# Two neighbouring rows of w_out to a partition, and every second column of w_in as the stationary operand

## The chip, the cores and the metric

The kernel runs on one core of one Trainium2 chip. The metric is the device time of one execution in microseconds (us). The time before is the median of five runs.

## What is computed

The first half is a gated linear attention over a sequence of 768, for 4 × 8 batches and heads of width 48; its output, as 3072 tokens of 384 numbers, goes through a two-layer perceptron with a squareplus in the middle. The change touches the perceptron only:

```python
# q, k, v, f_logit: (4, 8, 768, 48) float32; w_in: (384, 2048); w_out: (2048, 384)
f = 1.0 / (1.0 + np.exp(-f_logit))
for t in range(S):
    state = f[:, :, t, :, None] * state + np.einsum('bhd,bhe->bhde', k[:, :, t], v[:, :, t])
    y[:, :, t] = np.einsum('bhd,bhde->bhe', q[:, :, t], state)
x = y.transpose(0, 2, 1, 3).reshape(B * S, H * D)      # (3072, 384)
h = x @ w_in                                           # (3072, 2048)
g = 0.5 * (h + np.sqrt(h * h + 4.0))
out = g @ w_out                                        # (3072, 384)
```

## The kernel before

**Tiles of work.** The 3072 tokens are cut into 12 tiles, p = 0 to 11, of 256 tokens, three tiles to a batch. A tile has two halves, cc = 0 and 1, of 128 tokens. For each tile the kernel loads f, q, k and v (line 175), builds decay factors from f (exponentials, logarithms and cumulative sums with line 284's and 290's matmuls), scales q and k into a tile `qk` of fp16 (the products of line 142), transposes it into `qkT` (TensorE's line 391 for the first tiles, a transposing transfer at line 374 for tiles 4 to 11), computes scores (line 415), masks them into `pm` (line 430), updates the state (lines 443, 453, 469) and adds up the attention's output `y` in PSUM (lines 493, 502). `y` is copied to fp16 and transposed into `xT` (lines 517 or 526).

**First layer of the perceptron.** `xT` has for each half three blocks of 128 features by 128 tokens. The piece `m1.p.m` (line 542), for m = 0 to 7, computes 256 of the 2048 hidden columns: two groups, a = 0 and 1, of 128 columns each. A group is three matmuls that add up in PSUM; each has a 128x128 block of w_in as its stationary operand and 256 tokens as its moving operand. So a tile has 48 of these matmuls, all tiles 576, and each has a weight load of its own. The weights stand in four SBUF tiles `win`, of shape 128 x 3 x 512 in fp16, and group a takes the 128 contiguous columns from m % 2 * 256 + a * 128 on.

**Squareplus.** ScalarE squares h (line 551) and takes the root (line 557); VectorE adds half of h to it and writes the tile `g` (line 567), 128 hidden units to the partitions, 16 groups jn = 2m + a, 256 tokens.

**Second layer.** The piece `m2.p.cc n4` (line 579) runs four of the 16 groups jn; the 16 add up in one PSUM bank to 128 tokens by 384. The stationary operand is a 128x128 block of `g`, the moving operand the 384 columns of the 128 rows of w_out that belong to jn: `wout[jn // 2][:, jn % 2, :]`. There are 384 such matmuls. The result is copied to SBUF (`os`, line 139 on VectorE or line 137 on ScalarE) and stored (line 599).

**Weights.** w_in comes in four transfers of 384 KB of fp16 (line 148) and w_out in eight of 192 KB (line 153, pieces wo0 to wo7). Both are issued by GpSimd and turn float32 of memory into fp16 on the way. Transfer i of w_out brings rows 256 i to 256 i + 255: partition p gets row 256 i + p as j = 0 and row 256 i + 128 + p as j = 1. So a partition reads two runs of 384 numbers, 1536 bytes each, that lie 128 rows apart.

**What sets the order.** The order of all pieces is one list written out in the program, with the engine (and the PSUM banks) of each; on each engine the pieces run in that order. The loads of inputs, the transposing transfers and all stores but two of the last tile are issued from SP's queue in the list's order, so a store that waits for its data holds back the loads behind it. The w_out pieces stand in GpSimd's order between products and casts for tiles 2 to 5, and the first use of w_out is m2.0.00. Waits between pieces follow from the tiles that they read and write; buffers are reused in a ring of fixed depth for each name.

Of the kernel before, what the change touches and what calls it, by code (L numbers as in the profile page):

```python
# [126 lines left out]
def describe(nc, W, ctx_tiles, aps):  # L127
    q, k, v, f_logit, moe_w_in, moe_w_out, out = aps
    T, sb, ps, K = ctx_tiles
# [20 lines left out]

    for i in range(8):
        def wout(e, b, i=i):
            nc.gpsimd.dma_start(out=K["wout"][i], in_=moe_w_out[i * 256:(i + 1) * 256, :].rearrange("(j p) n -> p j n", p=128))

        W.add(f"wo{i}", "P", wout, makes=[f"wout{i}"], dma=("w", 1.26), cost={"P": 0.74})

    for p in range(NP):
        parts = [(0, 4), (4, 8)] if p in FINE else [(0, 8)]
        xs = range(len(parts))
        n = 384 // len(parts)  # L160
# [217 lines left out]
        if p not in XBAR:  # L378
            for x, (h0, h1) in enumerate(parts):
# [15 lines left out]
                for cc in range(2):  # L395
# [5 lines left out]
                    m = (j1 - j0) * 256  # L401
# [135 lines left out]
        for m in range(8):  # L537
            def m1(e, bk, m=m, p=p):
                T["h", p, m] = ps(bk[0], [128, 2, 2, 128], FP32)
                for a in range(2):  # L540
                    for j in range(NJ):
                        nc.tensor.matmul(out=T["h", p, m][:, a], lhsT=K["win"][m // 2][:, j, m % 2 * 256 + a * 128:m % 2 * 256 + a * 128 + 128],  # L542
                                         rhs=T["xT", p][:, :, j, :], start=(j == 0), stop=(j == NJ - 1))
            W.add(f"m1.{p}.{m}", "T", m1, reads=[f"xT{p}", f"win{m // 2}"], makes=[f"h{p}.{m}"], uses=[("xT", p)],
                  banks=[f"h{m}.{p}"], mode="F", cost={"T": 0.665})
            r, a = divmod(m, 2)

            def sq(e, bk, m=m, r=r, a=a, p=p):
                if ("hsq", p, r) not in T:
                    T["hsq", p, r] = sb("hsq", 4 * p + r, [128, 2, 512], FP16)  # L550
                nc.scalar.activation(out=T["hsq", p, r][:, a], in_=T["h", p, m].rearrange("p a c t -> p (a c t)"), func=AF.Square, scale=1.0)  # L551
            W.add(f"sq{p}.{m}", "A", sq, reads=[f"h{p}.{m}"], makes=[f"hsq{p}.{r}"], uses=[("bank", f"h{m}.{p}"), ("hsq", 4 * p + r)],
                  cost={"A": 0.585})
            if a == 1:
                def rt(e, bk, r=r, p=p):
                    T["r16", p, r] = sb("r16", 4 * p + r, [128, 2, 512], FP16)
                    nc.scalar.activation(out=T["r16", p, r], in_=T["hsq", p, r], func=AF.Sqrt, scale=0.25, bias=1.0)  # L557
                W.add(f"rt{p}.{r}", "A", rt, reads=[f"hsq{p}.{r}"], makes=[f"r16{p}.{r}"], uses=[("hsq", 4 * p + r), ("r16", 4 * p + r)],
                      table="s", cost={"A": 1.065})

        for m in range(8):
            r, a = divmod(m, 2)
# [167 lines left out]
```

## Time and profile before

| | |
|---|---|
| median of 5 runs | 196.72 us (196.11 to 200.51) |
| the profiled execution's own time | 197.05 us |
| its span, from the first to the last instruction | 194.8 us |
| granted TensorE clock, mean of the span | 0.987 |
| TensorE matmuls busy, of the span | 174.2 us |
| VectorE, ScalarE, GpSimd busy | 152.2, 156.0, 117.7 us |
| packets of transfers, bytes | 80505, 32.87 MB |
| of these from GpSimd's queue | 3872, 3.34 MB |
| w_out, from issue to landing | 7.1 us (median of 8) |

PE is TensorE's matmuls and PEld its weight loads, DVE is VectorE, ACT ScalarE, POOL GpSimd and SP SyncE, which only issues transfers; a q behind an engine's name is its instruction queue. A matmul's recorded duration runs from its start to the end of the pipeline, so durations of neighbouring matmuls overlap: the pace of a stream is the difference of the starts. The same holds for weight loads. A wait for several things is put down to the one that came last.

### The profile page before, as it was taken

The numbers are of one execution on the slowest core, as the hardware profiler recorded it, in microseconds if no ns is written. First come the engines' busy times: TensorE is split into PE (matmuls) and PEld (weight loads), VectorE is DVE, ScalarE is ACT, GpSimd is POOL, SyncE is SP. The second block draws the span as 40 slices with busy tenths as digits, with TensorE's granted clock in tenths as the row PEclk, the third lists the DMA queues.
The fourth block names the chain that finished last, engine by engine and source line by source line (L and its number), as shares of the span: only waits on it lengthen the run. The fifth ranks groups of instructions, "written<-read, shape, count | busy, mean of one in ns | idle before, by whom it ended". The sixth has DMA issues, their size and how long they took to land.

```text
span 194.8 us, 5593 instructions
## 1 busy us (share of the span) xinstructions
PE 174.2 (89%) x2287; PEld 125.7 (65%) x2287; DVE 152.2 (78%) x278; ACT 156.0 (80%) x250; POOL 117.7 (60%) x150
## 2 busy tenths in 40 slices
PE   0359997989999999899999899999987999999990
PEld 0236764767667766787677667777755777777660
DVE  5699869999989998779988978789755885664540
ACT  4568689899999979979999888997757779779800
POOL 5329889899999867787987999399700100000020
PEclk9999998799999999999999999999999999999998
DMA  5999999999968999999999979991989083000605
GB/s 141 276 260 249 234 242 247 215 254 246 201 151 196 211 201 242 197 261 225 230 190 227 129 142 227 200 205 28 96 141 184 3 69 89 13 0 0 162 13 152
DMA packets 80505, 32.87 MB, mean 169 GB/s; under 512 B 73888, under 2 KB 80448, under 8 KB 80480
## 3 DMA queue, kind: packets, MB, share of 16 engines
q1 hardware_dynamic: 76608, 29.17, 76.3%
q0 software_dynamic: 3872, 3.34, 10.6%
q8 instruction: 18, 0.29, 0.7%
q14 instruction: 7, 0.06, 0.1%
HBM read 25.17 MB, written 4.72 MB: 153 GB/s over the span
## 4 chain that ended last, share of the span: by engine, by line
PE 55%; DMA 12%; DVE 11%; POOL 8%; issue 4%; ACT 4%; SPq 3%; DVEq 0%; POOLq 0%
PE ps L579 22%; PE ps L542 20%; DVE pm L430 4%; DMA q<-in_q_dram 3%; DMA k<-in_k_dram 3%; POOL qk L142 3%; DMA v<-in_v_dram 2%; DMA xT<-y 2%; PE ps L493 2%; DVE g L567 2%; PE ps L391 2%; DMA out_dram<-os 2%; PE ps L415 2%; PE ps L284 2%; PE ps L502 2%
## 5 line engine op out<-in xcount | busy, mean ns | idle before, releaser
L542 PE MATMUL ps<-xT,win 128*128 128x256 f16 x576 | 75.6, 278 | 2.3 <-DVE os L139 0.9
L567 DVE SCALAR_TENSOR_TENSOR g<-ps,r 128x512 f16<-128x512 f32 x96 | 62.2, 682 | 15.1 <-ACT r L557 15.0
L579 PE MATMUL ps<-wout,g 128*128 128x384 f16 x384 | 71.4, 326 | 0.1
L551 ACT ACTIVATE hsq<-ps 128x512 f16<-128x512 f32 x96 | 54.1, 592 | 16.7 <-PE ps L542 16.3
L542 PEld LDWEIGHTS <-win 128*128 128x128 f16 x576 | 55.5, 99 | 15.1 <-issue 1.7
L557 ACT ACTIVATE r<-hsq 128x1024 f16<-128x1024 f16 x48 | 50.7, 1057 | 2.3 <-DVE g L567 1.0
L579 PEld LDWEIGHTS <-g 128*128 128x128 f16 x384 | 36.3, 98 | 19.8 <-issue 0.4
L430 DVE TENSOR_TENSOR pm<-ps,mask 128x512 f16<-128x512 f32 x48 | 31.1, 682 | 6.3 <-PE ps L415 6.2
L142 POOL TENSOR_TENSOR qk<-q,ea 128x384 f16<-128x384 f32 x22 | 22.6, 1049 | 0.2
L599 POOL DMA_DIRECT2D out_dram<-os x2 | 1.1, 576 | 35.2 <-DVE os L139 35.2
L142 POOL TENSOR_TENSOR qk<-k,ep 128x384 f16<-128x384 f32 x18 | 17.6, 997 | 0.2
L142 POOL TENSOR_TENSOR UT<-UT 128x384 f32<-128x384 f32 (+1 forms) x11 | 11.4, 1041 | 8.3 <-DVE UT L232 8.2
L284 PE MATMUL ps<-hl,tri 128*128 128x384 f16 (+1 forms) x34 | 9.1, 377 | 6.6 <-ACT hl L259 5.5
L142 POOL TENSOR_TENSOR sn<-st,gs 128x384 f16<-128x384 f32 x6 | 5.0, 829 | 14.0 <-DVE st L469 11.8
L142 POOL TENSOR_TENSOR k<-k,UT 128x768 f32<-128x768 f32 x7 | 12.6, 1813 | 0.0
L182 ACT ACTIVATE f<-f 128x768 f32<-128x768 f32 (+1 forms) x13 | 10.1, 793 | 2.9 <-DMA f<-in_f_logit_dram 2.9
L139 POOL CAST v<-v 128x768 f16<-128x768 f32 x9 | 7.8, 864 | 7.6 <-DMA v<-in_v_dram 7.6
L142 POOL TENSOR_TENSOR q<-q,UT 128x384 f32<-128x384 f32 (+1 forms) x10 | 9.8, 975 | 3.5 <-DMA q<-in_q_dram 3.5
L139 DVE COPY os<-ps 128x384 f32<-128x384 f32 x14 | 7.6, 551 | 4.2 <-DMA out_dram<-os 2.3
L415 PE MATMUL ps<-qkT 48*64 48x128 f16 x384 | 8.8, 227 | 0.9 <-DMA qkT<-qk 0.8
L232 DVE TENSOR_SCALAR UT<-f 128x768 f32<-128x768 f32 (+1 forms) x13 | 8.5, 657 | 1.0 <-ACT f L182 0.8
L284 PEld LDWEIGHTS <-tri 128*128 128x128 f16 x34 | 3.4, 112 | 8.8 <-DVE tri L655 3.6
(71 smaller groups left out, 204.3 us busy)
## 6 DMA issues: line engine op xcount, KB each, us to landing
f<-in_f_logit_dram SPq DMA_DIRECT2D x11, 384.0 KB, 5.5
k<-in_k_dram SPq DMA_DIRECT2D x11, 384.0 KB, 6.3
q<-in_q_dram SPq DMA_DIRECT2D x11, 384.0 KB, 6.1
v<-in_v_dram SPq DMA_DIRECT2D x11, 384.0 KB, 5.8
out_dram<-os SPq DMA_DIRECT2D x22, 192.0 KB, 3.5
win<-in_moe_w_in_dram POOLq DMA_DIRECT2D x4, 384.0 KB, 7.6
wout<-in_moe_w_out_dram POOLq DMA_DIRECT2D x8, 192.0 KB, 7.1
f<-in_f_logit_dram SPq DMA_DIRECT2D x2, 192.0 KB, 2.8
```

Of the source, the lines that this page charges most:

```text
L139: eng(e).tensor_copy(out=o, in_=i)
L142: eng(e).tensor_tensor(out=o, in0=a, in1=b, op=ALU.mult)
L182: nc.scalar.activation(out=t, in_=t, func=AF.Exp, scale=-1.0)
L232: eng(e).tensor_scalar(out=T["UT", p][:, 0::2, hs], in0=T["f", p][:, hs].rearrange("p h i d -> p i h d"), scalar1=1.0, scalar2=None, op0=A ...
L284: nc.tensor.matmul(out=T["cum", p, m][:, h0 * D:h1 * D], lhsT=tri[:, m], rhs=t[:, hs, 0:D], start=(r == 0), stop=(r == len(terms) - 1), sk ...
L415: nc.tensor.matmul(out=T["sc", p, i, h][64 * cc:64 * cc + 64, j, :], lhsT=t[r, 1, j, i, :], rhs=t[r, 0, j], start=True, stop=True)
L430: eng(e).tensor_tensor(out=T["pm", p, i, h], in0=T["pc", p, i, h] if key in PMACT else T["sc", p, i, h], in1=K["mask"][:, i].unsqueeze(1). ...
L542: nc.tensor.matmul(out=T["h", p, m][:, a], lhsT=K["win"][m // 2][:, j, m % 2 * 256 + a * 128:m % 2 * 256 + a * 128 + 128], rhs=T["xT", p][ ...
L551: nc.scalar.activation(out=T["hsq", p, r][:, a], in_=T["h", p, m].rearrange("p a c t -> p (a c t)"), func=AF.Square, scale=1.0)
L557: nc.scalar.activation(out=T["r16", p, r], in_=T["hsq", p, r], func=AF.Sqrt, scale=0.25, bias=1.0)
L567: nc.vector.scalar_tensor_tensor(out=T["g", p][:, 2 * m:2 * m + 2, :].rearrange("p a t -> p (a t)"), in0=T["h", p, m].rearrange("p a c t - ...
L579: nc.tensor.matmul(out=T["o", p, cc], lhsT=T["g", p][:, jn, cc * 128:(cc + 1) * 128], rhs=K["wout"][jn // 2][:, jn % 2, :], start=(jn == 0 ...
```

## The change

The loading of w_out gives partition p the rows 256 i + 2 p and 256 i + 2 p + 1, as r = 0 and 1. The two rows are neighbours in memory, so a partition reads one run of 3072 bytes. The SBUF tile keeps its shape, and line 579 is as before. So that the hidden units on the partitions of `g` are those of the rows of w_out, group a of the first layer takes every second of the 256 columns of w_in, from column a on, in place of 128 contiguous ones. The order of the pieces, the engines, the buffers and the loading of w_in stay.

```diff
     for i in range(8):
         def wout(e, b, i=i):
-            nc.gpsimd.dma_start(out=K["wout"][i], in_=moe_w_out[i * 256:(i + 1) * 256, :].rearrange("(j p) n -> p j n", p=128))
+            nc.gpsimd.dma_start(out=K["wout"][i], in_=moe_w_out[i * 256:(i + 1) * 256, :].rearrange("(p r) n -> p r n", r=2))
...
                 for a in range(2):
                     for j in range(NJ):
-                        nc.tensor.matmul(out=T["h", p, m][:, a], lhsT=K["win"][m // 2][:, j, m % 2 * 256 + a * 128:m % 2 * 256 + a * 128 + 128],
+                        nc.tensor.matmul(out=T["h", p, m][:, a], lhsT=K["win"][m // 2][:, j, m % 2 * 256 + a:m % 2 * 256 + 256:2],
                                          rhs=T["xT", p][:, :, j, :], start=(j == 0), stop=(j == NJ - 1))
```

## The prediction

> **What bounds the kernel now.** I read the page's shares and slices first, then TensorE's waits, then the groups of lines 542 and 579, then the transfers. The page (second and third lines: 40 slices of 4.87 us, busy tenths):
>
> ```profile
> PE 174.2 (89%) x2287; PEld 125.7 (65%) x2287; DVE 152.2 (78%) x278; ACT 156.0 (80%) x250; POOL 117.7 (60%) x150
> ...
> PE   0359997989999999899999899999987999999990
> ...
> DMA  5999999999968999999999979991989083000605
> ```
>
> TensorE is the resource to watch from slice 4 to slice 38; the transfers fill their 16 engines until about slice 25 and are idle more and more after that. Who TensorE waited for between 58 and 184 us (total, times, longest):
>
> ```profile
> PE ps L542 <- DVE os L139: 0.9, 1, 0.9
> PE ps L415 <- DMA qkT<-qk: 0.8, 1, 0.8
> PE ps L542 <- DMA xT<-y: 0.7, 1, 0.7
> PE ps L443 <- POOL v L139: 0.6, 1, 0.6
> PE ps L443 <- DVE pm L430: 0.2, 1, 0.2
> ```
>
> That is 3.2 us in 126. So from 58 us on the time is the sum of the matmuls, and nothing that only arrives earlier can win more than these 3.2 us. In the chain of waits, 12 matmuls of line 542 back to back take 1.31 us, 109 ns each, and 8 of line 579 take 1.30 us, 162 ns each. 576 × 109 + 384 × 162 = 62.8 + 62.2 = 125.0 us of the span. The 278 and 326 ns that the groups list are one matmul from start to modelled end; the pace is what counts.
>
> Next, whether the weight load that the change touches is hidden. The answers for line 542, and the timeline at 125 us and at 47 us (start, length, engine, instruction, count):
>
> ```profile
> L542 PEld LDWEIGHTS <-win x576: 95/98/151, 22.4 to 182.9; 128*128 128x128 f16 x192
> L542 PE MATMUL ps<-xT,win x576: 269/273/421, 22.4 to 183.0; 128*128 128x256 f16 x192
> ```
>
> ```profile
> 125.39 0.58 PEld L542 LDWEIGHTS <-win 128*128 128x128 f16 x6
> ```
>
> ```profile
> 125.43 0.82 PE L542 MATMUL ps<-xT,win 128*128 128x256 f16 x6
> ...
> 47.38 0.34 PE L290 MATMUL ps<-ind,hl 128*128 128x3 f16 x8
> ```
>
> The six loads run from 125.39 to 125.97, their matmuls start at 125.43: the first load is 40 ns ahead, and every later load starts as the matmul before it starts, so it has about 107 of the 109 ns until its own matmul. Line 290 has eight matmuls of 3 columns, each with its own 128x128 load (98 ns recorded like the others); less the 164 ns of one, (0.34 - 0.164)/7 = 25 ns from one to the next. So the 98 ns are mostly latency, which a following load overlaps, and a contiguous load occupies the array's load path for 25 ns at most.
>
> Last, the w_out transfers. Software queue (packets, MB, share of the 16 engines) between 35 and 52 us (only w_out is on it) and between 17 and 33 us (only w_in), then the cost of an issue on GpSimd (min/median/max ns):
>
> ```profile
> q0 software_dynamic: 2176, 1.57, 60.5%
> ```
>
> ```profile
> q0 software_dynamic: 1600, 1.57, 60.3%
> ```
>
> ```profile
> L153 POOL DMA_DIRECT2D wout<-in_moe_w_out_dram x8: 719/724/755, 33.2 to 44.5; - x8
> ```
>
> ```profile
> L148 POOL DMA_DIRECT2D win<-in_moe_w_in_dram x4: 789/796/949, 14.8 to 26.0; - x4
> ```
>
> ```profile
> 51.77 1.10 SPq L175 DMA_DIRECT2D k<-in_k_dram  x1
> 56.37 0.73 SPq L599 DMA_DIRECT2D out_dram<-os  x1
> ```
>
> ```profile
> 52.00:54.00 2.00, 2.00 (x16) 1.44 (x15) 2.00 (x4) 2.00 (x4) 2.00 (x3) 1.00 0.82 214
> 54.00:56.00 2.00, 2.00 (x30) 1.37 (x29) 1.41 (x4) 1.94 (x6) 1.98 (x3) 1.00 0.91 226
> 56.00:58.00 2.00, 2.00 (x29) 1.17 (x27) 2.00 (x3) 1.96 (x5) 2.00 (x3) 1.00 0.14 35
> ```
>
> In the last two of these (SP's timeline; busy time by stretch, whose last two columns are the share of the transfer engines and GB/s) the reader sees SP's queue stand from 52.9 to 56.4 us before a store of the output, and the transfers run dry at 56 us while TensorE works on (2.00 of 2.00 us).
>
> [...]
>
> **The change, part by part.** *Packets of w_out.* Each of the eight transfers has 256 packets now (1536 bytes of float32 read, 768 of fp16 written) and 128 after. 17 us × 0.605 × 16 engines / 2048 data packets = 80 ns a packet (the 128 others counted in it); for w_in, 16 us × 0.603 × 16 / 1536 = 100 ns at 2048 bytes read. That is 20 ns for 512 bytes, so about 140 ns at 3072 (estimate). 2048 × 80 / 16 = 10.2 us of all engines becomes 1024 × 140 / 16 = 9.0 us: 1.2 us less, between 35 and 52 us. Bounds: nothing (140 becomes 160, if a packet costs only by its bytes) and 3 us (a larger fixed part than I fitted).
>
> *Issue on GpSimd.* w_in has 384 packets and 796 ns an issue, w_out 256 and 724: 72 ns for 128 packets. Eight issues at about 650 ns save 8 × 72 = 0.58 us of GpSimd between 33.2 and 45.3 us; bounds 0 and twice that.
>
> *What of these reaches the end.* In that stage the chain runs over TensorE and VectorE, not over GpSimd or a transfer; no engine waits for a transfer between 35 and 57 us. TensorE's one listed wait there is 0.4 us, on VectorE. Loads of inputs that land a microsecond earlier meet SP's wait at 52.9 to 56.4 us, and the lead is gone when the transfers run dry. GpSimd's 0.58 us can shorten VectorE's turn of work a little. I take 0.4 us in all: two thirds of the GpSimd gain, nothing of the transfers. Bounds 0 and 1.7 us, see the second case.
>
> *The stationary operand.* 576 loads in line 542 step by 2 instead of 1; the number of loads, the matmuls, the moving operand and the PSUM tiles stay. If a load's occupation doubles from 25 to 50 ns it still fits into 107. Cost: nothing, hidden by the matmul before it. Without that cover each ns of overrun costs 576 ns on TensorE's path. Bounds: below nothing is excluded, because the pace of 109 ns is that of the moving operand; above, see the third case. The seam from line 579 to 542 has 162 ns of cover. At the half clock of 33 to 36 us the matmuls take about twice as long and so does the cover.
>
> *Second product.* Line 579 reads row r of a partition where it read block j; the moving operand is still 384 contiguous elements, and the row it meets is that of g. Cost nothing. No step is moved, and no wait is added: w_out is still eight transfers at the same places of GpSimd's order.
>
> Sum: 197.05 (the profiled execution; span 194.8 and 2.25 around it) - 0.4 - 0 + 0 = 196.65. That execution lies 0.33 above the median of 196.72, so set against the median I forecast 196.3.
>
> **The rivals.** *Second case, the relief gets through:* the loads keep their lead, SP's later entries move with it, and the waits on GpSimd's v (0.6) and on xT (0.7) fall away, with 0.4 from GpSimd's issues: 196.72 - 1.7 = 195.0. For it: transfers fill the engines in nearly every slice to 25, and both waits hang on chains through loads of q and v. Against it: the dry spell at 56 us, and waits of TensorE that begin 23 us and more later.
>
> *Third case, slower, the strided load is not hidden:* place, line 542, all of it on TensorE's path; it decides as soon as a load needs over 107 ns before its matmul, and 1.7 ns beyond make 1 us. [...] For it: no strided load in this trace, and 98 of 107 ns is little room if it is the record that counts. Against it: line 290 goes at 25 ns with the same record, and line 502 runs eight loads with 96-column matmuls in 0.51 us, (0.51 - 0.206)/7 = 43 ns each, far below its 98.
>
> *Fourth case, slower by arrival:* [...] f and v land later in the middle of the stage; 1.2 us later, uncovered, is 197.9. Against it: nobody waits for these loads before 57 us.
>
> That the packets don't merge at all gives 196.7, inside the first case.
>
> **How the numbers follow.** First case 0.57 (own range 195.8 to 197.2), second 0.23 (194.6 to 195.7), third 0.13 (197.8 to 250: above, twice the record's 98 ns would be 89 over, 51 us), fourth 0.07. The range 194.6 to 198.0 leaves out most of the third case and little else. A difference of 0.5%, 1 us, is about what the measurement can tell from no change. Faster by more: nearly all of the second case and a little of the first, 0.24; slower by more: third, fourth and a sliver of the first, 0.21; within: 0.55.
>
> **What would show it.** Line 542: 6 matmuls in 0.66 us, 12 in 1.31; a pace over 110 ns is the third case. The recorded load may grow from 98 ns without harm as long as the pace stays. w_out's issue: about 650 ns; the software queue: 1024 fewer packets, and about 1.2 us less of all engines. The dry spell at 56 us starts earlier, and SP's store is still late. If the time falls by over a microsecond, waits of TensorE at 80, 108, 143 or 148 us must have shrunk, and I misjudged how leads are lost.

## The result and the profile after

The changed kernel takes 198.96 us (median of 28 runs) where the kernel before takes 197.01 (47 runs). The medians are 1.95 us apart. The ratio is 1.0079 with a 95% interval of 1.0055 to 1.0102: slower, by about 1.6 us. This ratio, like each one below, leaves out of both kernels the executions counted as slow (about 1.5% above the fastest), so it can be smaller than that of the medians. Forecast were 196.3 us, a change too small to tell from none, and a range up to 198.0.

The single executions tell more than the median. Those of the kernel before lie between 195.4 and 201 us with two exceptions (203.1 and 840.86), three quarters of them below 198.5 (35 of 47). Of the changed kernel's, 19 of 28 are above 198.5 (one of them at 586.56), and none is below 196.1. The profiled execution of the changed kernel, 197.13 us, is the second fastest of the 28, so its profile hardly shows the loss. It does show whether the single steps of the forecast held. The page, slices of 4.87 us and the software queue over the whole span, changed kernel:

```profile
PE   0359996989999999999799899999998999999990
...
DMA  5999999999839999999989999893799073000605
...
q0 software_dynamic: 2848, 3.34, 9.7%
```

1024 packets fewer than the 3872 before: the rows do merge. The issue of w_out on GpSimd, line 542 (min/median/max ns), and twelve of its matmuls in the chain of waits, changed kernel:

```profile
L153 POOL DMA_DIRECT2D wout<-in_moe_w_out_dram x8: 528/546/594, 33.0 to 43.7; - x8
```

```profile
L542 PEld LDWEIGHTS <-win x576: 96/98/151, 22.4 to 182.8; 128*128 128x128 f16 x192
L542 PE MATMUL ps<-xT,win x576: 269/273/421, 22.4 to 182.9; 128*128 128x256 f16 x192
```

```profile
63.73 1.31 PE ps L542 x12
```

The load of every second column has the record of the contiguous one, 98 ns in the median and 151 at most in both, and so have its matmuls; twelve of these still take 1.31 us, 109 ns each. The issue has become 178 ns shorter (724 to 546), eight of them 1.4 us. Who TensorE waited for (total, times, longest; two lines of the start, which stand ahead of these in both kernels, are left out), and TensorE's stretches with the transfers' share and GB/s in the last columns, changed kernel:

```profile
PE ps L542 <- DMA xT<-y: 2.0, 2, 1.2
PE ps L284 <- DVE g L567: 1.5, 1, 1.5
PE ps L542 <- DVE os L139: 0.8, 1, 0.8
PE ps L542 <- DVE pm L430: 0.6, 1, 0.6
```

```profile
52.00:54.00 2.00, 2.00 (x23) 1.47 (x22) 2.00 (x5) 2.00 (x4) 2.00 (x3) 1.00 0.91 234
54.00:56.00 2.00, 2.00 (x29) 1.33 (x28) 1.18 (x3) 1.75 (x5) 1.98 (x3) 1.00 0.42 110
56.00:58.00 2.00, 2.00 (x29) 1.26 (x29) 2.00 (x4) 1.98 (x5) 2.00 (x3) 1.00 0.04 8
```

The transfers run dry about 1.4 us earlier than before (110 GB/s where it was 226), and SP's store still starts at 56.70 us (56.37 before). So the lead is lost there, as forecast. No row of this profile shows a large loss. It had to be looked for in executions that have it.

### The profile page after: what moved, and what is told of

Read it like the earlier page. It is cut to its first block, busy times and chain, and to the rows that moved or that the text cites. A ratio compares the mean times of both kernels' runs of the same rounds, so it can differ in the third digit from the quotient of the medians.

```text
span 194.8 us, 5593 instructions
## 1 busy us (share of the span) xinstructions
PE 173.4 (89%) x2287; PEld 125.4 (64%) x2287; DVE 153.2 (79%) x278; ACT 156.0 (80%) x250; POOL 117.3 (60%) x150
## 4 chain that ended last, share of the span: by engine, by line
PE 69%; DVE 11%; DMA 10%; ACT 3%; SPq 2%; issue 2%; POOL 0%; DVEq 0%
PE ps L579 28%; PE ps L542 25%; DMA xT<-y 5%; DVE pm L430 3%; PE ps L493 3%; DMA k<-in_k_dram 3%; PE ps L415 3%; PE ps L443 2%; DVE g L567 2%; PE ps L391 2%; PE ps L502 2%; DVE qk L142 2%; PE ps L284 2%; DMA out_dram<-os 2%; PE ps L526 1%
## 5 line engine op out<-in xcount | busy, mean ns | idle before, releaser
L142 POOL TENSOR_TENSOR q<-q,UT 128x384 f32<-128x384 f32 (+1 forms) x10 | 10.7, 1068 | 2.9 <-DMA q<-in_q_dram 2.9
L137 ACT COPY os<-ps 128x384 f32<-128x384 f32 x10 | 4.7, 471 | 6.6 <-PE ps L579 6.6
```

What stands on the lines that cost most here:

```text
L142: eng(e).tensor_tensor(out=o, in0=a, in1=b, op=ALU.mult)
```

## The experiments

Two theories were open at first. The *stride* theory, B in the expectations: the operand with step 2 costs TensorE something. The other, A: the new loading of w_out re-times what follows. The first four runs take the change apart between these two. What they showed split A in two, and the later runs are about that. The *packet* theory, D: the larger packets disturb other transfers. The *collision* theory, C: GpSimd is done with its issues earlier, its products meet other instructions of VectorE than before, and VectorE, which heads TensorE's work there, is held up.

**e1_packets**, the loading of w_out alone, line 542 as before. (Hidden units and rows of w_out are then paired otherwise; the work is the same.)

```diff
-...rearrange("(j p) n -> p j n", p=128)
+...rearrange("(p r) n -> p r n", r=2)
```

> Only the loading of w_out changes (two neighbouring rows to a partition); the first layer keeps its contiguous columns, so the hidden units and the rows of w_out don't belong together: the second product runs over other pairs, with the same shapes. Theory A, the w_out transfers re-time what follows: the whole loss is here, 198.5 to 199.0 against 197.0. Theory B, the strided weight load costs: no change, 196.5 to 197.2.

Measured: 199.68 us (6 executions), ratio 1.0118 (1.0058 to 1.0178).

**e2_stride**, the operand of line 542 alone, likewise.

```diff
-lhsT=K["win"][m // 2][:, j, m % 2 * 256 + a * 128:m % 2 * 256 + a * 128 + 128]
+lhsT=K["win"][m // 2][:, j, m % 2 * 256 + a:m % 2 * 256 + 256:2]
```

> Only the stationary operand changes (every second column); w_out is loaded as before, so the pairs of the second product differ from the reference's, with the same shapes. Theory A: no change against the kernel before, 197.0, and line 542 at 109 ns a matmul. Theory B: 198.5 to 199.0.

Measured: 196.36 us (22 executions), ratio 0.9988 (0.9960 to 1.0016).

**e3_both** and **e4_neither**, the changed kernel and the kernel before once more, as a measure for the other two.

> The changed kernel once more, for a profile of a typical execution beside the other three on one chip. Both theories: about 198.6 by time. Theory A: more waiting of TensorE between 60 and 152 us than the 3 to 4 us of the profile that lay at 197.13. Theory B: the same waits and a longer pace of line 542.

> The kernel before once more, for a second profile and the scatter of its times on this chip. Both theories: 197.0, ratio 1.00 within 0.3%; if single runs scatter by 2 us or more, one profile can't show where 1.5 us went, and only timed runs can.

Measured: 199.23 us, 1.0115 (1.0076 to 1.0155), and 196.69 us, 0.9984 (0.9957 to 1.0011). The stride costs nothing that can be told from zero, the loading of w_out has the whole loss.

Where it can arise is seen in e1's profiled execution (201.73 us, the slowest of the six). VectorE's timeline (start, length, engine, line, instruction, count), first of the kernel before and then of e1_packets:

```profile
40.70 0.67 DVE L430 TENSOR_TENSOR pm<-ps,mask 128x512 f16<-128x512 f32 x1
41.30 0.71 DVE L267 TENSOR_TENSOR hl<-s,hl 128x384 f16<-128x384 f32 x1
41.94 0.68 DVE L430 TENSOR_TENSOR pm<-ps,mask 128x512 f16<-128x512 f32 x1
```

```profile
40.64 0.68 DVE L430 TENSOR_TENSOR pm<-ps,mask 128x512 f16<-128x512 f32 x1
41.24 4.18 DVE L267 TENSOR_TENSOR hl<-s,hl 128x384 f16<-128x384 f32 x1
45.35 0.68 DVE L430 TENSOR_TENSOR pm<-ps,mask 128x512 f16<-128x512 f32 x1
```

One subtraction of 128x384, 0.55 to 0.8 us elsewhere in these two kernels, takes 4.18 us, and the mask behind it in VectorE's queue (line 430, for which TensorE waits) comes 3.4 us later. That one subtraction is 10.2% of the chain between 33 and 58 us. GpSimd beside it, kernel before and then e1_packets:

```profile
40.02 1.44 POOL L153 DMA_DIRECT2D wout<-in_moe_w_out_dram  x2
41.48 2.36 POOL L142 TENSOR_TENSOR qk<-q,ea 128x384 f16<-128x384 f32 x2
43.79 1.47 POOL L153 DMA_DIRECT2D wout<-in_moe_w_out_dram  x2
```

```profile
39.97 1.06 POOL L153 DMA_DIRECT2D wout<-in_moe_w_out_dram  x2
41.03 1.97 POOL L142 TENSOR_TENSOR qk<-q,ea 128x384 f16<-128x384 f32 x2
42.94 1.12 POOL L153 DMA_DIRECT2D wout<-in_moe_w_out_dram  x2
44.08 0.92 POOL L267 TENSOR_TENSOR hl<-s,hl 128x384 f16<-128x384 f32 x1
```

The issues ahead of them are shorter (two take 1.06 us instead of 1.44), so the two products (the piece qm3) begin at 41.03 instead of 41.48, and VectorE's subtraction, at 41.24, now comes after their start. It stands until 45.4 us: through both products, two issues and GpSimd's own line 267. In the kernel before VectorE came 0.18 us ahead, and it was GpSimd's pair that took longer, 2.36 us instead of 1.97. The price on TensorE, a stretch of the kernel before and then two of e1_packets:

```profile
40.00:46.00 6.00, 5.51 (x79) 4.65 (x79) 6.00 (x11) 5.92 (x8) 5.96 (x8) 1.00 1.26 240
```

```profile
40.00:46.00 6.00, 2.96 (x26) 2.44 (x25) 6.00 (x6) 5.78 (x7) 5.98 (x9) 0.96 1.18 239
46.00:52.00 6.00, 5.92 (x76) 4.28 (x76) 5.58 (x11) 3.13 (x5) 5.13 (x4) 0.75 1.08 248
```

TensorE is busy for 2.96 of 6 us (5.51 in the kernel before), and then its granted clock (the 0.75) is at half for 3.4 us. But e2's profiled execution (199.62 us, one of its slowest), with the old packets, has the same: 3.60 us at 41.78, with GpSimd's products at 41.96. VectorE and GpSimd of e2_stride:

```profile
41.78 3.60 DVE L267 TENSOR_TENSOR hl<-s,hl 128x384 f16<-128x384 f32 x1
```

```profile
41.96 1.97 POOL L142 TENSOR_TENSOR qk<-q,ea 128x384 f16<-128x384 f32 x2
```

So the hold-up is also there without the new packets; what the change can alter is how often it comes. 0.18 us ahead is no safe lead: one execution passed with it, another was held. The next runs move GpSimd in time without touching the packets, and the other way round.

**e5_both_pad**, the changed kernel with a product of 24 columns on GpSimd (0.24 us in the trace) behind each w_out issue. It gives back the time that the issues save; packets and operand stay changed. **e6_neither_pad** adds the same to the kernel before.

```diff
             nc.gpsimd.dma_start(out=K["wout"][i], in_=...)
+            h = K["half"].unsqueeze(1).unsqueeze(1).broadcast_to([128, 3, 4, 2])
+            nc.gpsimd.tensor_tensor(out=K["pad"], in0=h, in1=h, op=ALU.mult)
```

> The changed kernel with one product of 24 elements on GpSimd behind each issue of a w_out transfer (about 0.18 us each), so that GpSimd is again as late as in the kernel before while the packets stay at 3072 bytes. Theory C, the shorter issue lets GpSimd reach its products of line 142 before VectorE reaches its subtraction of line 267, which is then held up for 3 to 4 us in more of the executions, and re-times the rest: the loss goes, 196.5 to 197.3. Theory D, the larger packets themselves re-time the loads of the inputs: the loss stays, 198.5 to 199.3.

> The kernel before with the same eight small products on GpSimd: GpSimd 1.4 us later than before by 45 us, packets of 1536 bytes. Theory C: no worse than before, 196.2 to 197.2, and VectorE's subtraction never held up, since it comes well ahead of GpSimd's products. Theory D: no change, 196.7 (0.3% either way). Slower by over 1 us would say that GpSimd's later place costs by itself, and would spoil the reading of the padded changed kernel.

Measured: e5 196.14 us, 1.0004 (0.9980 to 1.0029), and e6 197.37 us, 1.0060 (1.0035 to 1.0084). With more work on GpSimd the changed kernel loses its whole loss, and the scatter too: its 22 runs lie between 195.03 and 197.33. The plain packet theory falls with it, since e5 has the large packets. What e5 doesn't separate is their spacing, because it also sets the issues as far apart as they were. But in the profiles of after, e1 and e3 no engine is listed as waiting for a transfer between 30 and 58 us. VectorE and GpSimd in e5_both_pad (its line 269 is line 267):

```profile
40.53 0.55 DVE L269 TENSOR_TENSOR hl<-s,hl 128x384 f16<-128x384 f32 x1
...
43.58 0.55 DVE L142 TENSOR_TENSOR q<-q,UT 128x384 f32<-128x384 f32 x1
```

```profile
41.34 1.95 POOL L142 TENSOR_TENSOR qk<-q,ea 128x384 f16<-128x384 f32 x2
```

VectorE leads by 0.81 us, and nobody is held. e6 missed what was expected: it is 1.03 us slower than the kernel before beside it, and its expectation says that over 1 us would spoil the reading of e5. In e6 GpSimd is later than it ever was (its products start at 42.55 us), and that has a price of its own: TensorE waits 0.7 us for w_out in line 579. e5's start at 41.34, near those of the kernel before (41.48, and 40.86 in e4), and it has no such wait, so its reading stands. Between e6 and e5 lie 1.2 us; 0.7 of it is that wait, and which part the packets and which the shorter issues have isn't separated.

**e7_both_order**, the changed kernel with wo6 and wo7 issued ahead of qm3, so that the products come later. **e8_neither_early**, the kernel before with qm3 ahead of wo3, so that they come earlier with the old packets.

```diff
-... lo4.0:D wo3:P ia2.1:T m1.1.6:T@4 pm2.00:D qm3.0:P ...
+... lo4.0:D wo3:P ia2.1:T m1.1.6:T@4 pm2.00:D wo6:P wo7:P qm3.0:P ...    (e7)
+... lo4.0:D ia2.1:T m1.1.6:T@4 pm2.00:D qm3.0:P wo3:P ...                (e8)
```

> The changed kernel with the last two w_out issues (wo6, wo7) moved ahead of tile 3's product of q on GpSimd (qm3), so that this product starts about 1.1 us later, behind VectorE's subtraction. Theory C: VectorE's subtraction takes 0.6 to 0.7 us in nearly all executions, and the time is 196.3 to 197.3. Theory D: 198.5 to 199.3.

> The kernel before, packets of 1536 bytes, with qm3 one place earlier on GpSimd, ahead of the issue wo3: the product starts about 0.7 us earlier, as in the changed kernel (41.0 us there, 41.5 before). Theory C: the held-up subtraction comes often, 198 to 200. Theory D: no change, 196.7.

Measured: e8 198.92 us (6 executions), 1.0101 (1.0032 to 1.0170): a loss of the same size without the change. But its profile doesn't show how. Line 267 goes free there (0.65 us), and what is caught is another instruction, a cast; VectorE and GpSimd of e8_neither_early:

```profile
38.72 2.15 DVE L139 CAST hl<-s 128x384 f16<-128x384 f32 x1
```

```profile
37.99 1.48 POOL L153 DMA_DIRECT2D wout<-in_moe_w_out_dram  x2
39.47 0.52 POOL L139 CAST hl<-s 128x384 f16<-128x384 f32 x1
39.91 0.72 POOL L153 DMA_DIRECT2D wout<-in_moe_w_out_dram  x1
```

This cast stands through the rest of two issues, a cast and a third issue. So the issues count among what it stands behind, not the products alone. All of these lie ahead of the piece that e8 moved (its products start at 40.65 us), so this hold-up can't come from the move. e8 supports the collision theory by its time alone.

e7 missed what was expected (196.3 to 197.3): 200.24 us (6 executions), 1.0146 (1.0076 to 1.0217). Line 267 goes free there (0.73 us), and the next instruction of the kind, the product q of line 142, takes 2.67 us at 44.36 us beside GpSimd's line 267 and its product k. The collision was moved on, not removed.

**e9_pad_5_3** and **e10_pad_6_7**: e5's product behind two of the issues only, to see which of the two meetings decides.

```diff
+            if i in (5, 3):      (e9; e10: (6, 7))
+                h = ...
+                nc.gpsimd.tensor_tensor(out=K["pad"], in0=h, in1=h, op=ALU.mult)
```

> The changed kernel with the small product of 0.18 us behind two of the w_out issues only, wo5 and wo3, the last two ahead of tile 3's product of q: that product and all that follows on GpSimd start 0.36 us later. Theory C1, the race is between that product and VectorE's subtraction (line 267) at 41 us: the loss goes, 196.2 to 197.2. Theory C2, the race is between GpSimd's line 267 at 44 us and VectorE's product of q (line 142): partly better, 197 to 198. Theory D: 198.5 to 199.3.

> The changed kernel with the small product behind wo6 and wo7 only, so that GpSimd is as early as in the changed kernel up to 43 us and 0.36 us later from there. Theory C1: the loss stays, 198.5 to 199.5, with VectorE's subtraction held up for 2 us or more in many executions. Theory C2: 196.2 to 197.2. Theory D: 198.5 to 199.3.

Measured, 6 executions each: e9 199.34 us, 1.0141 (1.0091 to 1.0190); e10 200.93 us, 1.0233 (1.0182 to 1.0285). Both missed. e9 comes close to the time that the packet theory named (up to 199.3), and e10 is slower than any theory had it. Neither half is enough, and a shift of under 0.4 us at the wrong place can be worse than none, as e10 shows. The profiles, though, show the hold-ups. e9's shows the price without the clock, since it and e5's have the full clock until 178 us (they are the slowest of e9's executions and the fastest of e5's, so their distance is more than that of the medians). TensorE around the hold-up (in brackets the idle time before, and what ended it), e5_both_pad and then e9_pad_5_3:

```profile
44.37 0.50 PE L504 MATMUL ps<-sn,qkT 128*128 128x96 f16 x8
...
49.65 0.64 PE L393 MATMUL ps<-ident,qk 64*128 64x64 f16 x32
```

```profile
44.58 0.82 PE L545 MATMUL ps<-xT,win 128*128 128x256 f16 x6 [1.83 <-DVE pm L433]
...
47.03 0.50 PE L505 MATMUL ps<-sn,qkT 128*128 128x96 f16 x8
...
52.62 0.64 PE L394 MATMUL ps<-ident,qk 64*128 64x64 f16 x32
```

VectorE's subtraction starts 0.21 us later in e9 than in e5 (40.74 and 40.53) and takes 3.19 us; the same eight matmuls start 2.66 us later, the transposes 2.97 us. That lag stays. Of the 4.7 us between the two spans, the other 1.7 come later, where e9 waits longer for `qkT` and `xT`. In e10 VectorE's subtraction is held for 1.42 us at 40.38, and then q for more; VectorE and GpSimd of e10_pad_6_7, and TensorE's stretch behind it:

```profile
44.11 3.15 DVE L142 TENSOR_TENSOR q<-q,UT 128x384 f32<-128x384 f32 x1
```

```profile
44.17 0.91 POOL L270 TENSOR_TENSOR hl<-s,hl 128x384 f16<-128x384 f32 x1
45.04 1.80 POOL L142 TENSOR_TENSOR k<-k,UT 128x768 f32<-128x768 f32 x1
```

```profile
46.00:52.00 6.00, 4.08 (x23) 2.31 (x23) 4.41 (x7) 2.71 (x4) 4.75 (x4) 0.58 1.13 257
```

The half clock now lasts from 47.0 to 53.8 us: 23 matmuls in 6 us.

**e11_four_ahead**, the changed kernel with four of these products ahead of wo1 and none behind the others: the delay of e5 in one piece, early. **e12_lo4_pool**, the changed kernel with the subtraction lo4 given to GpSimd, ahead of qm3, so that VectorE has none there.

```diff
+            if i == 1:
+                h = ...
+                for _ in range(4):
+                    nc.gpsimd.tensor_tensor(out=K["pad"], in0=h, in1=h, op=ALU.mult)    (e11)
```

```diff
-... lo4.0:D wo3:P ia2.1:T m1.1.6:T@4 pm2.00:D qm3.0:P ...
+... wo3:P ia2.1:T m1.1.6:T@4 pm2.00:D lo4.0:P qm3.0:P ...    (e12)
```

> The changed kernel with four small products in a row ahead of wo1 and none elsewhere: GpSimd 0.7 us later from 38 us on, with no gaps between the issues. Delay is what helps: 196.2 to 197.2. If instead the short products helped because VectorE slips in between them, the loss stays: 198 to 199.3.

> The changed kernel with tile 4's subtraction (lo4, line 267) on GpSimd, ahead of qm3, in place of VectorE: VectorE has 0.57 us less in this stage and meets GpSimd's product with no instruction that can be held up there. Theory C1: 195.8 to 197.0, and no executions of 200. Theory D: 198.5 to 199.3. If GpSimd's 0.9 us more are on the path, 197.5 to 198.5.

Measured: e11 197.90 us, 1.0047 (1.0018 to 1.0076); e12 197.35 us, 1.0045 (1.0018 to 1.0073). Both win back a part, and both missed what the collision theory expected (up to 197.2 and 197.0, and no executions of 200 in e12, which has one of 199.96 and one of 200.36). In e11 line 267 goes free and in e12 VectorE has none, and in both q of line 142 is caught (2.33 us at 43.38, 1.61 us at 43.59). e11's q starts 0.1 us after GpSimd's products have ended (43.27) and stands through two issues and line 267, so an issue can also be what it is first caught by.

**e13_both_again** and **e14_both_third**, two more profiled executions of the changed kernel, since two of those at hand had no hold-up.

> The changed kernel, for one more profile. Theory C: where TensorE keeps its full clock around 32 us, VectorE is early and one of its instructions that work on SBUF alone (lines 139, 267, 142) takes 1.4 to 4 us between 38 and 47 us; where the half clock comes at 32 us, VectorE is late and may pass free. Theory D: no such instruction, and the loss lies in transfers alone.

> The same once more. Theory C: as for the run before it; over the profiles of the changed kernel every execution has either a held-up instruction between 38 and 47 us or the half clock at 32 us, and those with both are the slowest, 200 and more. Theory D: times near 199 with neither.

Measured, one execution each: 198.58 and 198.76 us (the kernel before, once beside them, took 201.41, so these times say nothing by themselves). Both are held in line 267, for 1.86 us at 42.26 and for 3.42 us at 40.33. e13 has the half clock around 32 us as well, and was expected at 200 or more for that. All profiled executions side by side, sorted by how far VectorE's line 267 starts ahead of GpSimd's product:

| execution | VectorE ahead by, us | line 267 took, us | q of line 142 took, us |
|---|---|---|---|
| e6, e11, e7, e5 | 1.66, 0.98, 0.83, 0.81 | 0.55, 0.63, 0.73, 0.55 | 0.98, 2.33, 2.67, 0.55 |
| e4 (before) | 0.65 | 0.57 | 0.81 |
| e9 | 0.23 (0.05 ahead of the added product) | 3.19 | 0.86 |
| e2 | 0.18 | 3.60 | 0.79 |
| before | 0.18 | 0.71 | 0.71 |
| e10 | -0.03 | 1.42 | 3.15 |
| e14 (changed) | -0.05 | 3.42 | 0.64 |
| e1 | -0.21 | 4.18 | 0.83 |
| e13, e3, after (changed) | -0.79, -0.81, -0.82 | 1.86, 0.64, 0.65 | 1.18, 0.96, 0.97 |

With 0.65 us or more VectorE is never held in line 267, but in two of those five, e7 and e11, it is held in q instead. Between 0.23 ahead and 0.21 behind it was in five of six. About 0.8 us behind, it comes near the end of the first of GpSimd's two products, which are some 0.98 us each: twice it got in between the two, once not. The two profiles of the kernel before have no hold-up, and of the four of the changed kernel two have one: too few to count how often it comes. (Line 267 of e8 is left out, because its cast was held first; e12 has no such instruction.)

## Why the prediction was wrong

**What bounds the kernel.** That the chain of the stage runs over TensorE and VectorE was read rightly from the profile before, and that nothing after 58 us can win much, too. From this the forecast took that GpSimd's times don't matter except as a small gain. That is the step that failed, in its words: "GpSimd's 0.58 us can shorten VectorE's turn of work a little. I take 0.4 us in all". The sign was wrong: the earlier GpSimd comes with a loss of about 1.6 us, and in e5, with GpSimd set back, the loss is gone. Here an engine off the chain held one on the chain without handing it anything (4.18 us for VectorE's subtraction in e1, 0.55 in e5). "No step is moved, and no wait is added" holds for the list of pieces and not in time. Six issues lie ahead of qm3. What the first two save is lost in a wait of GpSimd at 36 us (for `UT`, 1.14 us in after where it was 0.51), and the other four, at 178 ns each, make 0.71 us. The measured shift is of that size: the products start 0.67 us earlier in after than in the kernel before, and 0.58 us earlier in e14 than in e4. The hold-up that came with it stands in no list of waits of VectorE; it shows only as a long instruction.

One profile was too few for the chain, too. In e4, the kernel before at 195.03 us, the chain does run over GpSimd and a transfer; pieces of it (start, length, what):

```profile
39.48 0.65 POOL wout L153
40.12 8.04 DMA wout<-in_moe_w_out_dram
...
48.20 1.14 PE ps L579 x6
```

TensorE waits 0.3 us for w_out there. So an earlier w_out can also be a gain in some executions.

**What was to be read beforehand.** The profile before had a sign of it: GpSimd's pair took 2.36 us, where three later ones (at 62.44, 75.13 and 93.57 us) take 1.95 or 1.96, at the very microsecond that the change moves. Caught in the runs were line 267 (two inputs in SBUF, up to 4.18 us in e1), line 142's q (two as well, up to 3.15 us in e10) and line 139's cast (one input, in SBUF, 2.15 us in e8), and not lines 430 and 567, with an input in PSUM, whose means are 682 to 684 ns in every kernel here. The 4.18 us in e1 go on through five GpSimd instructions, two issues among them. By what the one engine holds the other isn't shown; the runs show the hold-up and who is caught.

**Packets.** Right in size: 140 ns estimated, 133 measured as the mean of the trace's packets of 3072 bytes (79 for those of 1536), and about 1.5 us less of all engines where 1.2 was forecast (between 35 and 52 us the software queue has 51.6% of the engines' time, 60.5% before). Nothing of this reaches the end by itself, as forecast: e5, with the new packets and GpSimd's time given back, is at 1.0004.

**Issue on GpSimd.** Mis-sized as well: 650 ns forecast, 546 measured, 1.42 us in all where 0.58 was forecast and 1.16 was the upper bound. The line through w_in and w_out gave 0.56 ns a packet; from 256 to 128 packets of the same tensor it is 1.39 ns.

**Stationary operand and second product.** Right. Line 542's records, its pace of 109 ns and e2's ratio of 0.9988 leave no room for the third case; line 579 has 326 ns a matmul in both profiles.

**Lost leads.** Right: the dry spell starts near 54.8 us where it started near 56.2, is longer than before, and SP's store is still late.

**Rivals.** The fourth case had the sign (197.9 against 198.96) and another mechanism, arrival of transfers; e5 keeps the packets and has no loss. That VectorE and GpSimd hold each other up was in none of the four cases. A rival that the forecast doesn't name is the clock: it falls to half after some hold-ups (in e1 for 3.4 us), and around 32 us in part of the executions (in the kernel before from 32.6 to 36.1 us). The mean granted clock of the changed kernel's executions (without the one at 586.56 us) is 0.9886, that of the kernel before, 47 executions beside e1, 0.9903. If TensorE sets the whole time, the difference times 195 us makes 0.3 us (an estimate), so the clock alone isn't the loss.

**What stays open.** The profiled executions of after and e3 have no hold-up over 1 us at 41 us and still 197.13 and 198.67 us; both lose TensorE time between 94 and 100 us (4.84 and 4.39 of 6 us busy, the kernel before 6.00), partly in a wait for `xT` that e5 has too. e8, with the old packets, has 4.87 there. So how much of this belongs to the change isn't settled, nor how much of the 1.6 us the hold-ups carry. In part of the profiled executions, with either packets, the clock is at half around 32 us, ahead of any w_out issue; what starts it wasn't found. The meetings lie about a microsecond later with it: line 267 is at 41.30 us in the kernel before, and at 40.21 in e4, which has the full clock there. Whether e5 is cured by the lead alone or also by the gaps between its issues isn't settled either: e11 has the lead and is cured in part. No version was found that is safely faster than the kernel before; e5 equals it.

## What to carry to other kernels

Before making GpSimd faster or slower, look in the timeline at which VectorE instructions with all operands in SBUF lie beside its products, casts and issues, and which of the two comes first by how much: such instructions were the ones caught here, for up to 4.18 us. A lead of 0.2 us went either way here, and one of 0.65 us or more was enough for that instruction, though in e7 and e11 the next one was held. A change that shifts GpSimd can be judged only with such meetings in view. Where a kernel's single executions scatter by more than the effect that is looked for, take several profiles before reading a cause.

## What was not expected of the hardware

- A VectorE instruction of 0.55 us took up to 4.18 us beside GpSimd, over five GpSimd instructions in a row. In other executions it got in between two of them.
- Which of the two engines gives way at a lead of 0.18 us differed between executions (0.71 and 3.60 us).
- At TensorE's gaps of 2.83, 2.24, 2.03 and 2.14 us between 42 and 48 us (e1, e2, e7, e14) the granted clock went to half for 3.4 us, at that of 2.51 us in e10 for 6.8 us, beginning between 0.9 us ahead of the gap's end and 1.2 us after it; in e9, with a gap of 1.83 us, it didn't. The half clock around 32 us lasted 3.4 us too, in the kernel before and in after. What decides whether and when it comes wasn't tried.
- An issue on GpSimd took 546, 724 and 796 ns for 128, 256 and 384 packets (the last is w_in's).
- A stationary operand with every second column of fp16 had the record of the contiguous one, 98 ns, and the same pace of its matmuls, 109 ns.
